# Two more gate masks of a block-sparse attention turned by transposing transfers, in a new instruction order

## The chip, the cores and the metric

The kernel runs on one core of one Trainium2 chip. The core has TensorE (matrix products), VectorE, ScalarE, GpSimd, and SyncE, which here only issues transfers; each works through its own instruction stream in order, and semaphores tie the streams together. Sixteen DMA engines move data. The metric is device time in microseconds; one execution was also profiled. On the pages PE is TensorE, PEld its weight loads, DVE VectorE, ACT ScalarE, POOL GpSimd and SP SyncE, and a q behind a name is an engine's sequencer or queue.

## The reference

The input is q, k and v of 4 batches, 8 heads, 768 positions and 64 dimensions, and two weight matrices, w_in (512 x 2048) and w_out (2048 x 512). First comes an attention in which each query sees only some blocks of 64 keys, and then a two-layer network with a tanh-approximated GELU:

```python
k_rep = k.reshape(B, H, n_blocks, block, D).mean(axis=3)
gate_scores = np.einsum('bhsd,bhnd->bhsn', q, k_rep)
gate_scores = np.where(causal, gate_scores, -1000000000.0)
own_block = pos // block
top_idx = np.argsort(gate_scores, axis=-1)[..., -top_k:]     # top_k = 3
# mask: the chosen blocks and the own block, and causal within
scores = scale * np.matmul(q, k.transpose(0, 1, 3, 2))
scores = np.where(mask, scores, -1000000000.0)
attn = softmax(scores)
out = np.matmul(attn, v)                                     # heads side by side: x, 3072 x 512
h = x @ w_in
g = 0.5 * h * (1.0 + np.tanh(c * (h + 0.044715 * h * h * h)))
return g @ w_out
```

## The kernel before, in words

**Tiles and stages.** The work goes in pairs of heads: pair p holds heads 2(p mod 4) and the next one of batch p div 4, so pairs 0 to 3 are batch 0, 4 to 7 batch 1, and so on to 15. `pre(p)` prepares a pair: k and q are turned so that the head dimension lies in the partitions, k is summed by blocks into `ks` and `ksb`, TensorE makes the gate scores (L700, "the gate product"), VectorE turns them by 32 x 32 blocks (L716), adds the causal term (L723), finds the third largest by MAX8 (L732), compares (L733), and writes the gate mask `madd` (L737), 128 queries by 10 groups of 64 columns, 12 of them used, in fp16. The mask must then be turned too, so that block numbers lie in the partitions; it is copied into rows 64 to 75 of `qT` (L370 or L366, `qT<-bank` or `qT<-mT`), under the 64 rows of q, and meets there a constant pattern in the same rows of `kT`. So the score product (L1060) adds the mask by itself. `heads(p)` makes scores (L1060), exponentials on ScalarE (L1073), the triangle of the diagonal blocks on GpSimd (L1087), and the product with v (L1099); VectorE normalises (L982, L983), and the result is turned into `xT`, by TensorE (L1002) or by a transposing transfer (L1007). Batch 0 is done by `heads2` with lines L877, L896, L922, L945, L963 and L964 for the same steps. For batch 0, k and q are turned by TensorE (L559, L566, with `ident` and `identk`, and copied from PSUM by L366 or L370); later pairs are turned on VectorE (L586) and summed there (L634).

Per batch follow two stages: `s1` (L1136, 384-column products of w_in, and GELU on ScalarE, L1148), and the product with w_out: `s2_plain` for batch 0 (L1336, 512 columns) and `s2` for the others (L1386, 256 columns, in the seven-product scheme of Strassen, with additions on VectorE, L1323 and L1435). Batch 3's first layer uses the seven-product scheme in part (L1225).

**Two ways to turn the mask.** In `pre`, for pairs from 4 on, a flag `byPE` chooses. With it, `mask` issues five transposes on TensorE (L770) into a PSUM bank, and the copies read PSUM. Without it, `mask_dma` (L777) issues one transposing transfer on SyncE's queue from `madd` into a tile `mT` of two buffers in SBUF, and the copies read that. Before, `byPE` holds for pairs 4 to 7, batch 1.

**Loads.** SyncE issues nearly all transfers. The 24 head loads of batch 0 (pairs 0 to 3, k, q and v, two heads each; L406, L441) come first, four of them on ScalarE's queue. GpSimd issues the weights (L474, converting to fp16): w_in behind a small copy (L472) that reads the last v of batch 0 and so waits for it, w_out later in GpSimd's order. SyncE then copies a marker out of w_in (L1581), which waits until w_in has landed, and goes on with the loads of pair 4 and later (L412, L406).

**What sets the order.** Nothing is scheduled while the kernel is built: `Plan.run` walks a written list `ORDER` of operation numbers (1661 that emit instructions), takes the buffer of each tile from a second list `BUFFER`, and, where an operation can go to more than one engine, the engine from a table `ENGINE`. Each engine gets its instructions in the order of the list. Costs and priorities stand beside each operation in the code, but have no effect here; they were for the search that wrote the lists. 34 dummy products on zeros (`warm`, L1538) are in the list as well; they write a PSUM bank that nothing reads.

Of the kernel before, what the change touches and what calls it, by code (L numbers as in the profile page):

```python
# [230 lines left out]
def kernel(  # L231
# [16 lines left out]
    HP = H // 2  # L248
# [295 lines left out]
    def pre(p):  # L544
# [255 lines left out]
        else:  # L800
            byPE = p < 2 * HP
# [752 lines left out]
    for p in range(HP):  # L1554
        pre(p)
# [85 lines left out]
```

## Time and profile before

| | |
|---|---|
| median of 3 runs | 250.69 us (250.57 to 252.19) |
| the profiled execution | 251.68 us, its span 250.0 us |
| granted TensorE clock, mean | 0.998 |
| TensorE busy | 244.1 us, 98% of the span, 2492 products |
| VectorE busy | 189.0 us, 76% |
| ScalarE busy | 178.1 us, 71% |
| GpSimd busy | 81.0 us, 32% |
| DMA | 33.01 MB, 132 GB/s in the mean |
| L770, all five-block turns of masks | 40 transposes, 3.8 us busy |
| L777, mask transfers of batches 2 and 3 | 8, issue 1.20 us in the median |

A row of a timeline gives start and length in microseconds from the span's start, the engine, the line and operation, what is written and read, how many, and in brackets the idle time ahead of it with the engine, tile and line that ended it. A row of a group gives the busy time, the mean of one in nanoseconds, and the idle time ahead. Products on TensorE overlap, so the start of a row is later than the end of the row before only where TensorE paused; the rate is read from start to start.

### The profile page before, as it was taken

Reading aid. Unit: us, or ns where it says so; the run is one execution under the profiler, and the core shown is the slowest. Engines: PE = TensorE matmul, PEld = TensorE weight load, DVE = VectorE, ACT = ScalarE, POOL = GpSimd, SP = SyncE. Lnnn points to the kernel's source line nnn. Section 1 sums busy time; section 2 is a strip of 40 time slices with the busy share of each in tenths; the row PEclk is TensorE's granted clock in tenths of the full one; section 3 lists DMA queues with packets and bytes.
Section 4 is the critical chain, followed back from the end, with each engine's and each line's share of the span. In section 5 each row is a group of like instructions: output and inputs, shape, how many; then the busy total and the mean of one; then the engine's idle time right before and its main releaser. Section 6 shows DMA issues by size and latency. Waiting matters only on the chain.

```text
span 250.0 us, 6442 instructions
## 1 busy us (share of the span) xinstructions
PE 244.1 (98%) x2492; PEld 170.0 (68%) x2492; DVE 189.0 (76%) x542; ACT 178.1 (71%) x226; POOL 81.0 (32%) x162
## 2 busy tenths in 40 slices
PE   8989999999999999999999999999999999999993
PEld 6757776554556666665778887665877887666883
DVE  3799861050999999997998997998968583677953
ACT  2898996553799999768899875677998937657300
POOL 8546670011225875041146542300246400000000
PEclk9999999999999999999999999999999999999999
DMA  6997799999996668999978958235510330010024
GB/s 181 230 208 149 123 215 177 215 186 156 149 190 115 124 116 145 190 192 241 178 142 144 222 115 157 73 29 143 146 46 19 105 118 1 18 69 0 4 84 168
DMA packets 130479, 33.01 MB, mean 132 GB/s; under 512 B 123056, under 2 KB 126480, under 8 KB 130448
## 3 DMA queue, kind: packets, MB, share of 16 engines
q1 hardware_dynamic: 126736, 28.01, 55.1%
q0 software_dynamic: 3136, 4.19, 10.1%
q10 hardware_dynamic: 576, 0.39, 0.6%
q8 instruction: 19, 0.31, 0.5%
q14 instruction: 12, 0.10, 0.1%
HBM read 27.26 MB, written 6.29 MB: 134 GB/s over the span
## 4 chain that ended last, share of the span: by engine, by line
PE 90%; DMA 5%; DVE 3%; ACT 0%; issue 0%; POOL 0%; DVEq 0%
PE wide L1136 24%; PE bank L1386 22%; PE wide L1060 11%; PE bank L1336 8%; PE bank L1099 6%; PE wide L1225 6%; DMA w_out<-in_moe_w_out_dram 5%; PE wide L877 2%; PE bank L700 2%; PE bank L1538 2%; PE bank L566 2%; PE bank L945 2%; PE bank L770 1%; PE bank L559 1%; DVE ks L605 1%; DVE sel L732 1%
## 5 line engine op out<-in xcount | busy, mean ns | idle before, releaser
L1136 PE MATMUL wide<-xT,w_in 128*128 128x384 f16 x416 | 74.2, 326 | 0.0
L1073 ACT ACTIVATE ats<-wide 128x896 f16<-128x896 f32 x72 | 62.7, 913 | 5.4 <-PE wide L1060 4.2
L1148 ACT ACTIVATE G<-wide 128x768 f16<-128x768 f32 x52 | 42.1, 810 | 29.3 <-PE wide L1136 28.5
L1136 PEld LDWEIGHTS <-w_in 128*128 128x128 f16 x416 | 39.7, 98 | 26.8 <-issue 1.8
L1087 POOL TENSOR_SCALAR_AFFINE_SELECT ats<-ats 128x256 f16<-128x256 f16 x72 | 30.8, 438 | 57.5 <-ACT ats L1073 56.9
L1060 PE MATMUL wide<-qT,kT 76*128 76x512 f16 (+3 forms) x192 | 38.6, 305 | 0.0
L586 DVE STREAM_TRANSPOSE s<-sd 128x768 f32<-128x768 f32 x24 | 23.3, 971 | 11.7 <-DMA sd<-in_k_dram 10.2
L1386 PE MATMUL bank<-w_out,G 128*128 128x256 f16 x216 | 31.6, 272 | 0.0
L1386 PEld LDWEIGHTS <-G 128*128 128x128 f16 x288 | 27.0, 98 | 5.7
L368 POOL CAST kT<-s 64x768 f16<-64x768 f32 x19 | 16.0, 843 | 38.6 <-DVE s L586 38.2
L1336 PE MATMUL bank<-w_out,G 128*128 128x512 f16 x96 | 27.3, 379 | 0.4 <-DMA w_out<-in_moe_w_out_dram 0.4
L1435 DVE TENSOR_TENSOR osb<-bank,osb 128x512 f32<-128x512 f32 (+1 forms) x38 | 22.2, 593 | 4.7 <-PE bank L1386 3.7
L1099 PEld LDWEIGHTS <-ats 128*128 128x128 f16 x504 | 21.8, 98 | 3.8 <-POOL v L368 0.2
L1060 PEld LDWEIGHTS <-kT 76*128 76x128 f16 x192 | 17.4, 97 | 10.0 <-issue 0.3
L1099 PE MATMUL bank<-v,ats 128*128 128x65 f16 x504 | 23.8, 194 | 0.0
L1386 PEld LDWEIGHTS <-XS 128*128 128x128 f16 x216 | 20.0, 97 | 4.0
L896 ACT ACTIVATE ats<-wide 128x1024 f16<-128x1024 f32 (+3 forms) x24 | 20.6, 916 | 2.7 <-PE wide L877 2.4
L1386 PE MATMUL bank<-TS,XS 128*128 128x256 f16 x144 | 21.6, 272 | 0.0
L366 ACT CAST qT<-s 64x768 f16<-64x768 f32 x18 | 14.8, 824 | 0.2
L368 POOL CAST v<-vsd 128x768 f16<-128x768 f32 x13 | 11.4, 880 | 10.2 <-DMA vsd<-in_v_dram 10.1
L983 DVE TENSOR_TENSOR xn<-bank,zr 128x384 f16<-128x384 f32 x24 | 13.4, 557 | 0.8
L732 DVE MAX8 sel<-sel 128x8 f32<-128x12 f32 x160 | 13.3, 157 | 0.6
(123 smaller groups left out, 348.0 us busy)
## 6 DMA issues: line engine op xcount, KB each, us to landing
out_dram<-osb SPq DMA_DIRECT2D x23, 256.0 KB
vsd<-in_v_dram SPq DMA_DIRECT2D x26, 192.0 KB
sd<-in_k_dram SPq DMA_DIRECT2D x48, 96.0 KB
sd<-in_q_dram SPq DMA_DIRECT2D x48, 96.0 KB
w_in<-in_moe_w_in_dram POOLq DMA_DIRECT2D x2, 1024.0 KB, 11.0
w_out<-in_moe_w_out_dram POOLq DMA_DIRECT2D x2, 1024.0 KB, 13.9
G<-in_k_dram SPq DMA_DIRECT2D x4, 192.0 KB
G<-in_q_dram SPq DMA_DIRECT2D x4, 192.0 KB
```

The costliest lines, as they stand in the source:

```text
L368: nc.gpsimd.tensor_copy(out=out, in_=in_)
L586: nc.vector.transpose(out=T[key + "T32", p], in_=T[key, p].rearrange("p t j -> p (t j)"))
L896: nc.scalar.activation(out=T["at", u][:, :, 0:n], in_=plan.buf[("st",) + u].rearrange("p (h w) -> p h w", h=2)[:, :, 0:n], func=AF.Exp, bi ...
L1060: nc.tensor.matmul(st[:, x:e], kT16[i][h][0:76, s0:s0 + 128], qT16[i][h][0:76, s0 + (x - cb):s0 + (e - cb)], start=True, stop=True)
L1073: nc.scalar.activation(out=T["at", u][:, 0:n], in_=plan.buf[("st",) + u][:, 0:n], func=AF.Exp, bias=0.0, scale=SCALE)
L1087: nc.gpsimd.affine_select(out=dg, in_=dg, compare_op=ALU.is_ge, fill=0.0, base=0, pattern=[[0, 2], [1, 128]], channel_multiplier=-1)
L1099: nc.tensor.matmul(pvv[:, qc, 0:65], at[:, cb + (qc - jc) * 128: cb + (qc - jc + 1) * 128], v16[i][:, jc, h, :], start=(gi == 0 and jc == ...
L1136: nc.tensor.matmul(hps[:, 512 * e:512 * e + HALF], w_in16[:, ci, (2 * j + e) * 128: (2 * j + e + 1) * 128], T["xT", b][:, ci, HALF * h:HAL ...
L1148: nc.scalar.activation(out=G[:, :, h, j, :], in_=plan.buf["hps", b, j, h].rearrange("p (e w) -> p e w", e=2)[:, :, 0:HALF], func=AF.Gelu_a ...
L1336: nc.tensor.matmul(plan.buf["ops", b, ti], G[:, f % 2, 2 * ti // NC, f // 2, ti % (NC // 2) * 128:ti % (NC // 2) * 128 + 128], w_out16[:, ...
L1386: nc.tensor.matmul(dst[:, HD * h:HD * h + HD], FACT[m][0][:, j, t * 128:(t + 1) * 128], FACT[m][1][:, j, :], start=(clear and j == 0), sto ...
L1435: nc.vector.tensor_tensor(out=dst(), in0=src(), in1=other(), op=ALU.add)
```

## The change

Pairs 6 and 7 leave the TensorE way: `byPE` now holds for pairs 4 and 5 alone.

```diff
@@ pre @@
         else:
-            byPE = p < 2 * HP
+            byPE = p < HP + 2
             if byPE:
                 m = add({PE: 0.3}, mask, [sel], pr, takes=("pre", ("mk", p, 0)))
             else:
                 go = add({SP: 1.3}, mask_dma, [sel], -50,
                          takes=("mT", ("mT", p)))
                 m = add({"DMA": 0.8}, lambda _: None, [go], pr, lag=6.0)
```

The three lists are new from the first entry to the last. (All lines behind the lists stand one lower in the new file: L1136 becomes L1135.) The first entries of each:

```diff
 ORDER = [
-    1892, 1, 18, 4, 2, 9, 1893, 0, 1894, 5, 1895, 1896, 1897, 1898, 15,
+    2, 3, 18, 1894, 0, 1895, 9, 1896, 1, 1897, 22, 1898, 1899, 1900, 1901,
...
 ENGINE = {
...
     "DVE": [
-        5, 56, 145],
+        2, 3, 5, 56, 61],
     "POOL": [
-        337, 587, 588, 648, 649, 709, 710, 974, 975, 1037, 1038, 1099, 1100,
-        1161, 1162, 1427, 1428, 1552, 1615]}
+        338, 587, 588, 649, 710, 711, 977, 1039, 1040, 1101, 1102, 1163,
+        1164, 1429, 1430, 1492, 1554, 1555, 1617]}
```

What the new lists make of the streams, counted in the plan's operations (an operation can be several instructions): TensorE 875 (877 before), VectorE 301 (291), ScalarE 213 (220), GpSimd 129 (132), SyncE 143 (141). Of the places that matter below:

| | before | after |
|---|---|---|
| L1136 products ahead of the first L1336 | 48 | 38 |
| dummy products ahead of the first L1136 / behind the first L1336 | 34 / 0 | 31 / 3 |
| GpSimd operations between the issue of w_in and of w_out | 8 | 2 |
| clearing of constants (L524 to L529) of pairs 0 and 1 | GpSimd | VectorE, ahead of the copy into `identk` (L290) |
| copies of turned q and k from PSUM, batch 0 | 13 on ScalarE, 3 on VectorE | 9 on ScalarE, 7 on VectorE |
| SyncE's first issues | k of pair 1, k of pair 0 | k and q of pair 1 (first halves), k of pair 0 |
| VectorE operations between pair 6's mask and its first copy into `qT` | 1 | 7 |
| the same for pair 7 | 1 | 6 |

307 rows, old and new, of tables (BUFFER, ENGINE, ORDER) are left out of this document.

## The prediction

> **What bounds the kernel now.** I read the page's first two parts, then the chain of work that ended last, then the busy time by stages, and then TensorE's timeline where the chain leaves TensorE.
>
> ```profile
> span 250.0 us, 6442 instructions
> PE 244.1 (98%) x2492; PEld 170.0 (68%) x2492; DVE 189.0 (76%) x542; ACT 178.1 (71%) x226; POOL 81.0 (32%) x162
> PE 90%; DMA 5%; DVE 3%; ACT 0%; issue 0%; POOL 0%; DVEq 0%
> ...
> 34.00 11.57 DMA w_out<-in_moe_w_out_dram
> 100.06 15.06 PE wide L1136 x92
> 230.03 16.20 PE bank L1386 x148
> ```
>
> The last three rows are pieces of the chain (start, length, what). TensorE has 90% of the chain, and one transfer has 5%: w_out, on which the chain leaves TensorE until 45.57. Whether TensorE had slack behind that point, the table by stages tells (length, then busy time of TensorE, its weight loads, VectorE, ScalarE, GpSimd, clock, DMA share, GB/s):
>
> ```profile
> 11.00:36.30 25.30, 24.61 (x439) 18.11 (x439) 22.28 (x86) 22.64 (x32) 15.36 (x26) 1.00 0.93 176
> 36.30:45.57 9.27, 8.95 (x80) 5.69 (x78) 1.47 (x4) 6.54 (x9) 0.66 (x2) 1.00 1.21 187
> 45.57:96.20 50.63, 50.59 (x457) 29.21 (x457) 35.69 (x103) 38.94 (x49) 19.99 (x37) 1.00 0.89 152
> 45.57:246.30 200.73, 200.59 (x1882) 138.54 (x1881) 158.58 (x416) 143.60 (x179) 56.40 (x103) 1.00 0.60 120
> ```
>
> From 45.57 to its last product at 246.30 TensorE is busy 200.59 of 200.73 us, at clock 1.00. A busy row is no proof of full rate, but the chain's long pieces give 15.06/92 = 0.164 us for a 384-column matmul and 16.20/148 = 0.109 us for a 256-column one, and the short pieces agree. So behind 45.57 the end is work divided by rate: **the span is the moment of the first w_out product, plus the TensorE work still to do then, plus a tail of 250.0 - 246.3 = 3.7 us**. I need three things of the change: TensorE work removed, work left at that moment, and whether new waits appear.
>
> **TensorE work removed.** The two mask turns of pairs 6 and 7 are five transposes each (L770); here each stands with its successor:
>
> ```profile
> 79.81 0.44 PE L770 MATMUL bank<-ident,madd 128*128 128x128 f16 x5
> 80.09 0.54 PE L1060 MATMUL wide<-qT,kT 76*128 76x512 f16 x2
> ...
> 87.90 0.44 PE L770 MATMUL bank<-ident,madd 128*128 128x128 f16 x5
> 88.19 0.59 PE L1336 MATMUL bank<-w_out,G 128*128 128x512 f16 x2
> ```
>
> Start to start, 0.28 and 0.29: **-0.57 us**, in a stage with no slack, so it counts in full.
>
> **The new order: work left at the first w_out product.** This is where I expect the change to be decided.
>
> ```profile
> 24.67 0.19 POOL L472 COPY after_in<-vsd 1x16 f32<-1x16 f32 x1 [0.72 <-DMA vsd<-in_v_dram]
> 34.00 1.78 POOL L474 DMA_DIRECT2D w_out<-in_moe_w_out_dram  x2
> 39.24 0.57 SPq L1581 DMA_DIRECT2D after_in<-w_in x1
> 36.30 0.81 PE L1136 MATMUL wide<-xT,w_in 128*128 128x384 f16 x4
> 45.61 0.38 PE L1336 MATMUL bank<-w_out,G 128*128 128x512 f16 x1 [0.36 <-DMA w_out<-in_moe_w_out_dram]
> ```
>
> GpSimd starts w_in when the last v of batch 0 has landed (24.67); w_in is whole by 39.24, where SyncE's marker copy that waits for it starts; the first half of w_out is there at 45.57. TensorE had waited 0.36 us. In the old order the first L1336 stands behind 48 L1136 matmuls, in the new one behind 38. Ten are left for afterwards: 10 x 0.164 = **+1.64 us**, if w_out lands when it did. And three of the 34 dummy matmuls (L1538, 256 columns), all ahead of the first L1136 before, now stand behind the first L1336, where nothing hides them: 3 x 0.109 = **+0.33**.
>
> When does w_out land? In the new GpSimd order its start stands two operations behind w_in's, not eight, so some 6 us earlier. But w_in's start still waits for the same last load, the 24 head loads ahead of it are the same bytes, and w_out was issued at 34.00, 5 us ahead of w_in's end, so its queue was not empty. What an earlier start could recover is a dip where w_in ends:
>
> ```profile
> 36.00:40.00 4.00, 4.00 (x53) 2.88 (x52) 1.39 (x4) 3.36 (x6) 0.81 (x2) 1.00 1.11 171
> 40.00:44.00 4.00, 4.00 (x29) 2.47 (x27) 0.36 (x1) 2.37 (x4) 0.00 (x0) 1.00 1.23 199
> ```
>
> 171 against 199 GB/s over 4 us is 0.56 us of transfer. Bounds 0 and -0.56 (a loss is excluded as long as the last v lands at its time); I take **-0.28**, the middle, since nothing shows what makes the dip: w_out at 45.3.
>
> Does TensorE get there by 45.3? Before, it arrived at 45.61 - 0.36 = 45.25; with ten matmuls fewer ahead that is 43.6. Against this, the opening got heavier on VectorE, which is busy 22.28 of 25.30 us there:
>
> ```profile
> 1.63 0.33 DVE L525 MEMSET madd<- 128x320 uint32 x1
> 2.01 0.19 DVE L529 MEMSET qT<- 12x64 uint32 x2
> 2.23 1.15 DVE L290 COPY identk<-ident 128x384 f32<-128x384 f32 x1
> 4.38 3.43 PE L566 MATMUL bank<-identk,G 128*64 128x128 f32 x36
> 22.04 0.55 DVE L370 COPY s<-bank 128x384 f32<-128x384 f32 x1
> 23.28 0.49 DVE L370 COPY XS<-bank 128x640 f16<-128x640 f16 x1
> 24.98 0.55 DVE L370 CAST v<-TS 128x768 f16<-128x768 f32 x1
> 28.36 0.28 DVE L737 SCALAR_TENSOR_TENSOR madd<-sel,ownm 128x120 f16<-128x120 f32 x1
> ```
>
> Until pair 3's gate mask (28.36) it now does four more 0.55 us copies of turned q and k, and one 0.49 copy and one 0.55 cast less: 2.20 - 1.04 = +1.16. It also clears two pairs' constants, once GpSimd's, ahead of the identk copy at 2.23. The one clearing that stands there now takes from 1.63 to 2.20, so two more are about 1.2 us; the copy then ends at 4.6 instead of 3.4, and L566 starts some 0.2 to 0.4 late. Together 43.6 + 1.16 + 0.4 = 45.1: just inside w_out's 45.3. So I let the transfer set the moment, with 0.2 us of cover; if that is gone, each further microsecond costs one (third rival).
>
> **The mask on SyncE.** What takes the place of the ten transposes:
>
> ```profile
> L370 DVE COPY qT<-mT 12x640 f16<-12x640 f16 x16 | 6.0, 374 | 0.5
> L370 DVE COPY qT<-bank 12x640 f16<-12x640 f16 x6 | 2.9, 484 | 0.3
> 108.00 1.20 SPq L777 DMA_TRANSPOSE mT<-madd x1
> 113.03 0.32 DVE L370 COPY qT<-mT 12x640 f16<-12x640 f16 x1
> L586 DVE STREAM_TRANSPOSE s<-sd 128x768 f32<-128x768 f32 x24 | 23.3, 971 | 11.7 <-DMA sd<-in_k_dram 10.2
> L634 DVE TENSOR_REDUCE ks<-s 128x12 f32<-128x768 f32 x12 | 11.2, 940 | 0.1
> L983 DVE TENSOR_TENSOR xn<-bank,zr 128x384 f16<-128x384 f32 x24 | 13.4, 557 | 0.8
> L982 DVE RECIPROCAL zr<-bank 128x6 f32<-128x6 f32 x24 | 4.5, 186 | 6.0 <-PE bank L1099 5.8
> L370 DVE CAST qT<-s 64x768 f16<-64x768 f32 x6 | 3.5, 584 | 0.1
> L716 DVE STREAM_TRANSPOSE sel<-bank 128x160 f32<-128x160 f32 (+2 forms) x17 | 5.6, 333 | 9.0 <-PE bank L700 8.8
> ```
>
> The copies into qT: three on VectorE and one on ScalarE from PSUM before (3 x 0.484 on VectorE), now four on VectorE from SBUF (4 x 0.374): VectorE +0.05, ScalarE one copy less. Neither sets the end in this stage (35.69 and 38.94 busy of 50.63), so zero; if VectorE is the one that pair 7 waits for, it is 0.05. SyncE gets two issues of 1.20 us and, being in order, stops at each until VectorE has the mask: behind pair 6's stand the rest of k of pair 9, v of pair 7, k of pair 8; behind pair 7's the turning of pair 4's output, the second half of v of pair 7, q of pairs 8 and 9. These are loads for later work; I cost them at nothing, and if v of pair 7 came late its products on TensorE would wait.
>
> The turn's latency the trace does not show alone. From below it is the issue, 1.2 us; from above 5.0, since the copy at 113.03 follows the issue at 108.00 and did not wait. Between pair 6's mask and its first copy the new order has VectorE do two transposes, a reduction, a normalisation (L982 and L983), a cast and the gate's transpose: 2 x 0.971 + 0.940 + 0.743 + 0.584 + 0.333 = 4.5 us; for pair 7 it is two transposes, a reduction, two normalisations and a copy, 1.942 + 0.940 + 1.486 + 0.374 = 4.7. At 5.0 VectorE waits 0.5 and 0.3; at 1.2 not at all. The upper end is only a copy's place in a queue, so I take zero, and keep 0 to +0.8 for the range.
>
> The Trainium skill speaks against the change here: "VectorE: DVE Perf Modes", Rules for kernel authors, would have a 128x128 transpose on TensorE where PSUM will do, and the table of The three transpose paths gives 1309 ns for the DMA's against 390 ns for TensorE's. Five blocks at that price would be an estimated 6.5 us, and the row above shows at most 5.0 from issue to copy.
>
> **The sum**, against this execution's own span: 250.0 - 0.57 + 1.64 + 0.33 - 0.28 = 251.1, so +1.1 us. The order of the last operations is different, but ends as before in three half-products, one VectorE addition and a store, so the tail stays 3.7. The profiled execution took 251.68 (1.68 around its span); the three runs' median is 250.69, and I add the difference to that: **251.8 us**.
>
> **Rivals.**
>
> *Faster: the w_out wait dissolves.* If the last v landed earlier and both weights with it, by the 1.6 us that TensorE could be early, the ten matmuls would no longer be left over: -0.57 + 0.33 - 0.36 = -0.6, 250.1 us. It decides at w_out before about 44. For: the new order issues one more load before SyncE first has to wait, and w_out is asked for sooner. Against: the transfers are the same bytes at a DMA share near 0.93. A gain of 1% would need 2.5 us, which nothing here offers.
>
> *Slower in the opening.* Besides the 1.16, the new VectorE order puts both normalisations of pair 0 (0.74 each) ahead of pair 2's mask copy, where it had one; if VectorE has no pause to absorb this, pair 3's scores come up to 0.74 later still, plus ScalarE's gap. Arrival at 46.0 to 46.4 instead of 45.3, +0.7 to +1.1 on top: 252.5 to 252.9.
>
> *The mask is late.* If the turn takes all of the 5.0 us, and SyncE has another issue of 1.2 in hand when VectorE is done, the mask is there after 6.2: VectorE, in order, waits 1.7 and 1.5 us, and the first L1060 of the pair stands in TensorE's order with nothing to pass it. That gives up to 251.8 + 3.2 = 255.0, and 253.4 if half is covered. It decides at 4.5 us from mask to landing. For: every copy of the mask behind VectorE's other work. Against: the eight turns of batches 2 and 3 delayed no copy. The table of the skill named above would put it on this side too.
>
> *The change does not do what it says:* the instruction lists have ten L770 fewer and two DMA_TRANSPOSE more, so this has no chance.
>
> **How the numbers follow.** Forecast 0.52 (its own range 251.2 to 252.5); faster 0.17; slower opening 0.2; late mask 0.11. The range must leave out no more than 0.2, so it runs from 250.0, just under the faster rival, to 253.7, just over the late mask half covered. A measurement of this kernel can tell about 1% from no change: below 248.2 or above 253.2. Above lies most of the late mask and a little of the slow opening: 0.16. Below lies only what I have not seen: 0.04.
>
> **What would show it.** Right: the first L1336 again waits for w_out, longer than 0.36, at 45.0 to 45.6; then ten L1136 more between it and the gate products of pairs 8 and 9 at the end of the stage; L1386's last piece ends near 247.4; no wait of VectorE on mT, none of TensorE at pair 6 or 7. Wrong: w_out landing before 44 or after 46.5, a wait ahead of the first L1336 that names VectorE or ScalarE, or an idle stretch of TensorE behind it.

## The result, and the profile after

| | before | after |
|---|---|---|
| median | 251.75 us (250.57 to 252.56, 8 executions) | 253.03 us (252.53 to 253.97, 8 executions) |
| ratio after to before, 95% interval | | 1.0060 (1.0033 to 1.0087) |
| the profiled execution, its span | 251.68 us, 250.0 us | 253.59 us, 251.8 us |
| TensorE products | 2492 | 2482 |
| first w_out product, wait for w_out ahead of it | 45.61 us, 0.36 us | 45.23 us, 0.77 us |
| TensorE's end | 246.22 us | 247.48 us |
| remaining time: first w_out product to TensorE's end | 200.61 us | 202.25 us |
| tail: TensorE's end to the end of the span | 3.8 us | 4.3 us |

By the medians the change costs 1.28 us, by the ratio 0.6%; the prediction said 1.1. In the eight executions of this comparison the kernel before has its median at 251.75, not at the 250.69 of its first three, so what is compared is the difference; as an absolute time the 251.8 of the prediction is 1.2 low, inside its range of 250.0 to 253.7. The two profiled executions lie 1.9 us apart, further than the medians. The page of the changed kernel, its first line, the busy times and the chain by engine:

```profile
span 251.8 us, 6423 instructions
PE 244.1 (97%) x2482; PEld 168.9 (67%) x2482; DVE 196.1 (78%) x560; ACT 175.1 (70%) x219; POOL 76.0 (30%) x151
PE 79%; DMA 10%; SPq 5%; POOL 1%; ACT 1%; issue 1%; ACTq 0%; DVE 0%; POOLq 0%
```

Ten products fewer, the same busy time of TensorE, and a longer span. Next the table by stages (same columns as for the kernel before):

```profile
11.00:36.30 25.30, 24.89 (x432) 18.19 (x430) 22.49 (x89) 22.53 (x31) 14.41 (x25) 1.00 0.96 177
36.30:45.57 9.27, 8.50 (x86) 5.47 (x84) 2.59 (x6) 6.88 (x9) 0.73 (x2) 1.00 1.23 202
45.57:247.90 202.33, 201.82 (x1885) 139.00 (x1882) 163.84 (x422) 141.25 (x174) 54.67 (x103) 1.00 0.60 120
```

Behind 45.57 TensorE is as full as before; the 0.51 us of idle time in the last row are the 0.42 behind its last product and 0.09 in 202 us. So the reading "moment plus work left" still holds. VectorE's busy time in the opening, 22.49, is only 0.21 above the 22.28 of before, though three of the four further copies stand there (the fourth starts at 5.48). The places themselves, from the timelines of TensorE, GpSimd, SyncE and VectorE:

```profile
24.26 0.20 POOL L471 COPY after_in<-vsd 1x16 f32<-1x16 f32 x1 [0.68 <-DMA vsd<-in_v_dram]
27.86 1.78 POOL L473 DMA_DIRECT2D w_out<-in_moe_w_out_dram  x2
41.38 3.09 PE L1135 MATMUL wide<-xT,w_in 128*128 128x384 f16 x18
45.23 0.38 PE L1335 MATMUL bank<-w_out,G 128*128 128x512 f16 x1 [0.77 <-DMA w_out<-in_moe_w_out_dram]
48.59 0.27 PE L1537 MATMUL bank<-XS 128*128 128x256 f16 x1
78.78 1.33 SPq L776 DMA_TRANSPOSE mT<-madd  x1
83.55 0.32 DVE L369 COPY qT<-mT 12x640 f16<-12x640 f16 x1
85.89 1.25 SPq L776 DMA_TRANSPOSE mT<-madd  x1
90.44 0.67 DVE L369 COPY qT<-mT 12x640 f16<-12x640 f16 x2
244.91 2.57 PE L1385 MATMUL bank<-w_out,G 128*128 128x256 f16 x22
247.51 0.69 DVE L1434 TENSOR_TENSOR osb<-bank,osb 128x512 f32<-128x512 f32 x1 [0.23 <-PE bank L1385]
```

The first L1335 again waits for w_out, at 45.23; TensorE was there at 44.46. One of the three late dummies follows at 48.59. Each mask is copied 4.8 and 4.6 us behind its issue, and no bracket names `mT`. TensorE ends at 244.91 + 2.57 = 247.48, VectorE's last addition at 248.20.

The tail grew too. Table by stages, first of the kernel before, then of the one after, from about the end of the last store's packets to the end of the span:

```profile
248.55:250.00 1.45, 0.00 (x0) 0.00 (x0) 0.00 (x0) 0.00 (x0) 0.00 (x0) 0.61 0.01 1
```

```profile
249.85:251.80 1.95, 0.00 (x0) 0.00 (x0) 0.00 (x0) 0.00 (x0) 0.00 (x0) 0.50 0.00 0
```

No engine is busy and next to nothing is moved in either stretch (1 and 0 GB/s), and it is 0.5 us longer after. The fourteen profiles of this case, those of the experiments below included, speak against scatter between executions. The tail is 3.7 to 3.8 us in the two kernels that turn the masks of pairs 6 and 7 on TensorE (before, e2), 4.0 to 4.1 in those with the two further transfers and the old opening (e1, e3, e8, e9, e10, e12), and 4.3 to 4.5 in those with the transfers and the new opening (after, e4 to e7, e11). In e3, which differs from the kernel before in the turns alone, the transfers thus come with 0.3 us of tail. Why they do is open.

### The profile page after: what moved, and what is told of

The parts are those of the page before. It is cut to its first block, busy times and chain, and to the rows that moved or that the text cites. A ratio compares the mean times of both kernels' runs of the same rounds, so it can differ in the third digit from the quotient of the medians.

```text
span 251.8 us, 6423 instructions
## 1 busy us (share of the span) xinstructions
PE 244.1 (97%) x2482; PEld 168.9 (67%) x2482; DVE 196.1 (78%) x560; ACT 175.1 (70%) x219; POOL 76.0 (30%) x151
## 4 chain that ended last, share of the span: by engine, by line
PE 79%; DMA 10%; SPq 5%; POOL 1%; ACT 1%; issue 1%; ACTq 0%; DVE 0%; POOLq 0%
PE wide L1135 25%; PE bank L1385 22%; PE wide L1059 11%; PE bank L1335 8%; DMA w_out<-in_moe_w_out_dram 7%; PE bank L1098 6%; SPq L405 5%; PE wide L1224 5%; DMA vsd<-in_v_dram 2%; PE bank L699 2%; DMA G<-in_q_dram 2%; POOL w_in L473 1%; ACT ats L365 1%; ACT G L1248 1%; PE bank L1001 0%
## 5 line engine op out<-in xcount | busy, mean ns | idle before, releaser
L1135 PE MATMUL wide<-xT,w_in 128*128 128x384 f16 x416 | 74.6, 326 | 0.0
L1135 PEld LDWEIGHTS <-w_in 128*128 128x128 f16 x416 | 39.9, 98 | 27.4 <-issue 2.3
L1086 POOL TENSOR_SCALAR_AFFINE_SELECT ats<-ats 128x256 f16<-128x256 f16 x72 | 29.4, 419 | 58.0 <-ACT ats L1072 40.6
L1385 PE MATMUL bank<-w_out,G 128*128 128x256 f16 x216 | 33.1, 272 | 0.0
L1335 PE MATMUL bank<-w_out,G 128*128 128x512 f16 x96 | 28.4, 379 | 0.8 <-DMA w_out<-in_moe_w_out_dram 0.8
L1098 PE MATMUL bank<-v,ats 128*128 128x65 f16 x504 | 24.6, 194 | 0.0
L1385 PE MATMUL bank<-TS,XS 128*128 128x256 f16 x144 | 23.2, 272 | 0.0
L895 ACT ACTIVATE ats<-wide 128x1024 f16<-128x1024 f32 (+3 forms) x24 | 21.2, 916 | 2.2 <-PE wide L876 1.4
L367 POOL CAST v<-vsd 128x768 f16<-128x768 f32 x12 | 10.2, 852 | 11.0 <-DMA vsd<-in_v_dram 10.4
L365 ACT CAST qT<-s 64x768 f16<-64x768 f32 x16 | 13.1, 827 | 0.2
```

The lines of the kernel that those rows point to most:

```text
L367: nc.gpsimd.tensor_copy(out=out, in_=in_)
L895: nc.scalar.activation(out=T["at", u][:, :, 0:n], in_=plan.buf[("st",) + u].rearrange("p (h w) -> p h w", h=2)[:, :, 0:n], func=AF.Exp, bi ...
L1086: nc.gpsimd.affine_select(out=dg, in_=dg, compare_op=ALU.is_ge, fill=0.0, base=0, pattern=[[0, 2], [1, 128]], channel_multiplier=-1)
L1098: nc.tensor.matmul(pvv[:, qc, 0:65], at[:, cb + (qc - jc) * 128: cb + (qc - jc + 1) * 128], v16[i][:, jc, h, :], start=(gi == 0 and jc == ...
L1135: nc.tensor.matmul(hps[:, 512 * e:512 * e + HALF], w_in16[:, ci, (2 * j + e) * 128: (2 * j + e + 1) * 128], T["xT", b][:, ci, HALF * h:HAL ...
L1335: nc.tensor.matmul(plan.buf["ops", b, ti], G[:, f % 2, 2 * ti // NC, f // 2, ti % (NC // 2) * 128:ti % (NC // 2) * 128 + 128], w_out16[:, ...
```

## The experiments

In all of them "first w_out product", "remaining time" and "TensorE's end" are read as in the table above; the new files have the same code with line numbers five lower than the kernel after (L1330 for L1335). `ORDER` is quoted as the part of one engine. In the order lists 433 and 434 are the first two w_out products, 1925 to 1927 the late dummies, 163 the start of w_out. The medians come from several chips; each ratio is against the kernel before on the same chip. The full table, in microseconds:

| kernel | first w_out product | its wait | remaining | TensorE's end | median | ratio to before (95%) |
|---|---|---|---|---|---|---|
| e1 | 44.75 | 0 | 204.14 | 248.89 | 254.58 | 1.0127 (1.0103 to 1.0152) |
| e2 | 45.51 | 0.77 | 202.56 | 248.07 | 252.92 | 1.0067 (1.0048 to 1.0087) |
| e3 | 44.35 | 0 | 204.82 | 249.17 | 255.93 | 1.0195 (1.0156 to 1.0235) |
| e4 | 45.66 | 0 | 200.64 | 246.30 | 252.45 | 1.0052 (1.0036 to 1.0069) |
| e5 | 45.75 | 0.85 | 202.24 | 247.99 | 254.08 | 1.0117 (1.0097 to 1.0138) |
| e6 | 45.84 | 0 | 200.31 | 246.15 | 252.20 | 1.0037 (1.0023 to 1.0050) |
| e7 | 48.21 | 0 | 200.62 | 248.83 | 255.07 | 1.0152 (1.0133 to 1.0171) |
| e8 | 45.08 | 0.56 | 202.23 | 247.31 | 253.58 | 1.0100 (1.0074 to 1.0125) |
| e9 | 44.56 | 0.30 | 202.37 | 246.93 | 253.22 | 1.0086 (1.0063 to 1.0108) |
| e10 | 45.01 | 0 | 202.38 | 247.39 | 253.12 | 1.0079 (1.0060 to 1.0099) |
| e11 | 45.31 | 0 | 200.30 | 245.61 | 251.82 | 1.0028 (1.0016 to 1.0041) |
| e12 | 46.08 | 0 | 201.51 | 247.59 | 253.70 | 1.0112 (1.0092 to 1.0131) |

### e1: the old opening with the new order behind it

```diff
 ORDER = [
-    2, 3, 18, 1894, 0, 1895, 9, 1896, 1, 1897, 22, 1898, 1899, 1900, 1901,
+    1894, 1, 18, 4, 2, 9, 1895, 0, 1896, 5, 1897, 1898, 1899, 1900, 15, 1901,
...
```

The first 408 entries are those of the kernel before, through a w_out product near 56 us (operation 470); then come the changed kernel's entries that are left.

> The instruction order of the kernel before up to about 56 us (through its first w_out products), the changed kernel's order behind that, masks of pairs 6 and 7 turned by SyncE. Theory of the prediction (the moment of the first w_out product and the work left then set the end; the turns themselves are free): first L1335 at 45.6 with a wait of 0.36 as before, 48 L1135 ahead of it, TensorE's end 246.22 - 0.57 = 245.65, time 0.57 us under the kernel before (ratio 0.998). Rival (the loss sits in the order behind the opening or in the turns): TensorE's end near 247.5 as in the changed kernel, with a pause of TensorE or a wait on mT between 56 us and the end.

The first w_out product came earlier than expected (44.75 instead of 45.6) and without a wait for w_out, but the seam broke. TensorE's timeline, and the table by stages behind it:

```profile
68.73 0.48 PE L694 MATMUL bank<-s,ksb 128*32 128x160 f32 x8 [2.09 <-ACT qT L360]
69.10:73.70 4.60, 4.60 (x24) 2.36 (x21) 4.10 (x17) 3.25 (x5) 2.04 (x5) 0.63 0.86 158
```

TensorE stood for 2.09 us behind ScalarE's copy of a mask, and right behind that the granted clock was 0.63 over 4.6 us, which costs 4.6 x 0.37 = 1.7 us more. 200.04 + 2.09 + 1.7 = 203.8 of the 204.14 are thus accounted for. Neither theory is decided; e8 and e9 mend the seam.

### e2: the new opening with the old order behind it

```diff
-            byPE = p < HP + 2
+            byPE = p < 2 * HP
```

with the first 407 entries of the changed kernel's `ORDER` (through the same w_out product), and then what is left of the list of the kernel before.

> The other half: the changed kernel's order up to about 56 us, the order of the kernel before behind that, masks of pairs 6 and 7 turned by TensorE. Theory: first L1336 at 45.2 with a wait of 0.77 as in the changed kernel, TensorE's end 247.48 + 0.57 = 248.05, time 1.8 us over the kernel before (ratio 1.007), since the whole loss lies in the opening. Rival (loss behind the opening): TensorE's end near 246.2 to 246.6.

TensorE's timeline:

```profile
45.51 0.38 PE L1330 MATMUL bank<-w_out,G 128*128 128x512 f16 x1 [0.77 <-DMA w_out<-in_moe_w_out_dram]
245.29 2.78 PE L1380 MATMUL bank<-w_out,G 128*128 128x256 f16 x24
```

TensorE's end 248.07, expected 248.05. With everything else old, the new opening alone costs the time: 202.56 is 200.61 + 1.64 + 0.33, to 0.02. The second reading is less kind to the change: with the masks on TensorE and the old order the remaining time is only 0.31 above the 202.25 of the changed kernel, not 0.57.

### e3: the turns alone, in the old order

```diff
-            byPE = p < 2 * HP
+            byPE = p < HP + 2
```

with the order lists of the kernel before; each transfer stands right behind its mask.

> The order of the kernel before, only the masks of pairs 6 and 7 turned by SyncE; VectorE's first copy of each mask stays where it was, 0.9 us (pair 6) and 0.8 us (pair 7) behind the mask's end, so that VectorE's wait on mT measures the turn. Theory of the prediction (turn of 1.2 to 5.0 us, near 2.5 from issue to landing): VectorE waits about 1.7 us twice, TensorE's first L1060 of each pair comes 1.2 us late, TensorE's end 246.22 - 0.57 + 2.4 = 248.0. Rival short turn (1.2): no wait of TensorE, end 245.65. Rival long turn (5.0): VectorE waits 4.1 us twice, TensorE's end near 253.

Timelines of SyncE, VectorE and TensorE:

```profile
67.35 1.68 SPq L406 DMA_DIRECT2D sd<-in_k_dram  x3
78.36 1.31 SPq L771 DMA_TRANSPOSE mT<-madd  x1
80.75 3.62 SPq L406 DMA_DIRECT2D sd<-in_k_dram  x5
81.07 0.32 DVE L364 COPY qT<-mT 12x640 f16<-12x640 f16 x1 [1.85 <-DMA mT<-madd]
81.54 0.54 PE L1054 MATMUL wide<-qT,kT 76*128 76x512 f16 x2 [1.20 <-DVE qT L364]
89.21 1.21 SPq L771 DMA_TRANSPOSE mT<-madd  x1
90.03 0.79 PE L1093 MATMUL bank<-v,ats 128*128 128x65 f16 x21 [1.43 <-DVE xn L977]
91.62 0.32 DVE L364 COPY qT<-mT 12x640 f16<-12x640 f16 x1 [1.74 <-DMA mT<-madd]
92.08 0.92 PE L1054 MATMUL wide<-qT,kT 76*128 76x512 f16 x6 [1.26 <-DVE qT L364]
```

A turn takes 81.07 - 78.36 = 2.7 us and 91.62 - 89.21 = 2.4 us from issue to copy; VectorE waits 1.85 and 1.74 (expected 1.7), TensorE 1.20 and 1.26 at the first score products (expected 1.2). The third pause, 1.43, was not expected: VectorE, late by then, normalises late, and the bank is not free. The five loads of k that SyncE issues at 80.75 went out at 71.30 in the kernel before:

```profile
71.30 3.83 SPq L412 DMA_DIRECT2D sd<-in_k_dram  x5
```

SyncE is in order, and stood from 69.03 to 78.36 at a transfer whose mask did not exist yet. So the late mask is a real mechanism: it costs 4.2 us of remaining time (204.82 against 200.61) where nothing covers it. In time e3 came out uneven: two executions took 254.95 and 255.01, some 4.0 over the kernel before (250.95), and two took 256.85 and 257.64, with a mean granted clock of 0.985 instead of 1.000 and 0.998.

The table of the Trainium skill that the prediction cites ("VectorE: DVE Perf Modes", The three transpose paths) gives 1309 ns for one 128x128 block by DMA; five blocks landed here in 2.4 to 2.7 us, about 0.5 us a block, and the measurement decides.

### e4: the wait for w_out filled

```diff
-    390, 433, 391, 373, 434, 374, 375, 376, 393, 394, 395, 396, 1925, 403,
+    390, 391, 373, 374, 375, 376, 433, 393, 394, 395, 396, 434, 1925, 403,
```

> The changed kernel with its first two L1335 moved behind the matmuls that they stood behind in the kernel before (first one behind ten more L1135). Theory (ten L1135 are 1.64 us, the wait of 0.77 is filled): no wait for w_out, first L1335 at 46.1 instead of 45.23, TensorE's end 247.48 - 0.77 = 246.71, time 0.8 us under the changed kernel, so about 0.5 over the kernel before. Rival (something else sets TensorE's pace behind 45 us, ScalarE's gelus or the PSUM tiles): the wait reappears within the next 10 us under another name, TensorE's end 247.5.

TensorE's timeline:

```profile
45.66 0.38 PE L1330 MATMUL bank<-w_out,G 128*128 128x512 f16 x1
243.73 2.57 PE L1380 MATMUL bank<-w_out,G 128*128 128x256 f16 x22
```

The wait is gone and does not come back; the remaining time falls by 1.61 (expected 1.64), the end by 1.18 (0.77 expected; TensorE got there 0.4 earlier than in the profile of after). So the ten matmuls left over are the largest term of the remaining time, as predicted. The kernel is still 0.5% slower than before, and now its arrival sets the moment: 45.66 with 48 L1130 ahead, where the old opening arrived between 44.26 and 45.25 in before, e1, e3, e8 and e9 (first product less its wait).

The expected gain in time is not seen: the ratio is 1.0052 against 1.0060 for the changed kernel, with intervals that overlap, and the kernel is 1.5 us over the one before (250.95 on this chip), where 0.5 was expected; 0.5 of the 1.5 is its longer tail. The 1.64 of the ten matmuls can't come back in full. Put back ahead, they would bring the changed kernel's TensorE to w_out at 44.46 + 1.64 = 46.10, 0.85 behind the 45.25 of before; only the wait of 0.77 is there to be filled. So the wait for w_out had hidden that the new opening is late.

### e5: w_out asked for later

```diff
-    157, 231, 145, 163, 270, 265, 276, 285, 299, 304, 310, 319,
+    157, 231, 145, 270, 265, 276, 285, 299, 304, 163, 310, 319,
```

> The changed kernel, only GpSimd's start of the w_out transfer moved back behind the operations that it stood behind in the kernel before (about 34 us instead of 27.9). Step (d) of the prediction (the earlier start fills a dip of the DMA rate): w_out lands 0.3 to 0.4 later, first L1335 at 45.6 with a wait of about 1.1, TensorE's end 247.9. New theory (the two runs with the late start met no wait at 44.35 and 44.75, the three with the early start had w_out at 45.2 to 45.5: the earlier start makes the first half land later, because it shares the queues with w_in and the loads): w_out is there by 44.4, the wait of 0.77 shrinks below 0.2, first L1335 at 44.5, TensorE's end 246.8. No effect of the start: 45.2 and 0.77 as it was.

Timelines of GpSimd and TensorE:

```profile
35.33 1.78 POOL L468 DMA_DIRECT2D w_out<-in_moe_w_out_dram  x2
45.75 0.38 PE L1330 MATMUL bank<-w_out,G 128*128 128x512 f16 x1 [0.85 <-DMA w_out<-in_moe_w_out_dram]
```

Asked for 7.5 us later, w_out lands 0.52 later, and TensorE's end moves by 0.51 to 247.99 (expected 247.9 by step (d)). The ratio says more, 1.0117 against 1.0060, with intervals that do not meet. So the new theory, that an early start delays w_out, falls. How much the early start gains is not shown: the traces tell when the first half of w_out landed, also where TensorE did not wait for it, and that is 44.3 to 45.6 in the six other kernels that ask late (before, e1, e3, e8, e9, e12) and 44.3 to 45.5 in the seven that ask early (after, e2, e4, e6, e7, e10, e11), against 45.7 here.

### e6: without the late dummies

```diff
-    396, 434, 1925, 403, 404, 435, 405, 436, 418, 406, 419, 437,
+    396, 434, 403, 404, 435, 405, 436, 418, 406, 419, 437,
```

and 1926 and 1927 likewise; the rest is e4. The dummies' products are read by nobody.

> The kernel of e4, without the three dummy matmuls that stand behind the first w_out product. Step (c) of the prediction (nothing hides them there): from the first L1330 to TensorE's end 200.64 - 0.33 = 200.31 us. Rival (they fill pauses of TensorE, or hold its clock up): 200.64 unchanged, or longer at a clock below 1.00.

```profile
45.84 0.38 PE L1330 MATMUL bank<-w_out,G 128*128 128x512 f16 x1
243.59 2.56 PE L1380 MATMUL bank<-w_out,G 128*128 128x256 f16 x22
```

From these two rows of TensorE's timeline: 246.15 - 45.84 = 200.31, to the hundredth. The 0.33 are real, and the clock stays at 1.00 without them.

### e7: four copies back on ScalarE

```diff
     "ACT": [
-        63, 67, 74, 85, 90, 94, 99, 101, 105, 107, 119, 139, 331, 345, 348,
+        63, 67, 72, 74, 85, 90, 94, 99, 101, 105, 107, 110, 119, 121, 130, 139,
+        331, 345, 348, 486, 504, 523, 541, 595, 596, 598, 656, 657, 719, 753,
...
```

The rest is e4.

> The kernel of e4, four copies of turned q and k of pairs 0, 2 and 3 back on ScalarE, where the kernel before had them (VectorE 4 x 0.55 = 2.2 us less in the opening). In e4 TensorE reaches the first L1330 at 45.66 without a wait, in e1 and e3 with the old opening at 44.75 and 44.35: 0.9 to 1.3 earlier with the same work ahead. Theory of the prediction's step (e) (VectorE's load in the opening makes TensorE late): first L1330 at 44.5 to 44.9, and the end as much earlier, if w_out has landed; otherwise a wait for w_out up to 45.2 to 45.5. Rival (ScalarE is as full there, 22.5 of 25.3 us busy; or the loads set the pace): first L1330 at 45.5 or later.

TensorE's timeline:

```profile
19.21 0.68 PE L939 MATMUL bank<-v,ats 128*128 128x65 f16 x16 [0.95 <-ACT s L360]
30.30 0.41 PE L939 MATMUL bank<-v,ats 128*128 128x65 f16 x8 [1.35 <-ACT XS L360]
48.21 0.38 PE L1330 MATMUL bank<-w_out,G 128*128 128x512 f16 x1
```

2.5 us later, with pauses that name ScalarE's copies: in this order ScalarE has no room for them. What the four copies cost on VectorE the run does not tell, since it moved the load and did not take it away. The timelines tell more. From the first score product to TensorE's arrival at w_out, with 1.64 added where ten matmuls were left over, it is 33.7 to 34.3 us in six profiles of the old opening (before, e1, e3, e8, e9, e10) and 33.7 to 34.8 in six of the new one (after, e2, e4, e5, e6, e11). And the write of pair 3's mask, behind all these copies, starts at 29.56 in the changed kernel and at 28.36 in the one before: 1.20 late, where the first score product is already 1.22 late (e11). So behind the first score product the copies add nothing that can be seen.

### e8: the seam of e1, first mend

One engine entry of e1 (348, the second mask copy of pair 4) goes from ScalarE to VectorE.

```diff
     "ACT": [
-        63, 67, 72, 74, 85, 90, 94, 99, 101, 110, 119, 121, 130, 139, 345, 348,
-        349, 449, 486, 504, 523, 541, 595, 596, 598, 656, 657, 719, 753, 933,
+        63, 67, 72, 74, 85, 90, 94, 99, 101, 110, 119, 121, 130, 139, 345, 349,
+        449, 486, 504, 523, 541, 595, 596, 598, 656, 657, 719, 753, 933, 984,
...
```

> The kernel of e1, with one copy moved: at the seam of the two orders e1 had both mask copies of pair 4 on ScalarE, the second one behind the table load, and TensorE waited 2.09 us for it (68.73); here the second is on VectorE, as in the kernel before. Theory: no pause of TensorE behind the first w_out product, clock 1.00 throughout, from the first L1330 to TensorE's end 200.61 - 0.57 = 200.04 us, time 0.57 under the kernel before (ratio 0.998), 2 us under the changed one. Rival (the clock dip and the rest of e1's loss were not the pause's): 201 to 204 us as in e1 less 2.09.

```profile
68.83 0.48 PE L694 MATMUL bank<-s,ksb 128*32 128x160 f32 x8 [1.85 <-DVE qT L364]
```

TensorE's timeline shows the same pause under another engine's name: the two orders put pair 4's mask and pair 5's gate into one bank. The clock stayed at 1.00 here, so 200.04 + 1.85 leaves 0.34 of the 202.23. Of that, 0.27 is in the 96 L1330, which took 21.22 us instead of 20.95 in the kernel before (summed from start to start, pauses left out).

### e9: the seam, second mend

```diff
 BUFFER = [
...
-    0, 2, 3, 0, 0, 0, 4, 1, 1, 0, 3, 0, 1, 1, 5, 0, 2, 1, 2, 0, 1, 0, 0, 1, 0,
+    0, 2, 3, 0, 1, 1, 4, 0, 1, 1, 3, 0, 0, 0, 5, 1, 2, 0, 2, 0, 1, 0, 1, 1, 1,
...
```

Behind the seam, PSUM banks 0 and 1, and the two wide tiles, change places; otherwise e8.

> The kernel of e8 with the PSUM banks 0 and 1 (and the two wide tiles) exchanged behind the seam: in e8 and e1 the gate of pair 5 came into the bank of pair 4's mask, which the two orders had placed differently, and TensorE waited 1.85 and 2.09 us for the mask's copy. So this is at last the opening of the kernel before with the changed kernel's order and turns behind it. Theory: no pause of TensorE behind the first w_out product, from there to TensorE's end 200.61 - 0.57 = 200.04 us, time 0.57 under the kernel before (ratio 0.998). Rival (the changed order behind the opening is worse by itself): more than 200.6 us.

TensorE's timeline:

```profile
44.56 0.38 PE L1330 MATMUL bank<-w_out,G 128*128 128x512 f16 x1 [0.30 <-DMA w_out<-in_moe_w_out_dram]
67.79 0.48 PE L694 MATMUL bank<-s,ksb 128*32 128x160 f32 x8 [1.19 <-DVE s L580]
71.31 0.45 PE L764 MATMUL bank<-ident,madd 128*128 128x128 f16 x5 [0.48 <-DVE madd L731]
244.37 2.56 PE L1380 MATMUL bank<-w_out,G 128*128 128x256 f16 x22
```

The moment is the old one, and two pauses of 1.67 us in all are left at the seam, now behind VectorE. Without them the remaining time would be 200.70: the theory's 200.04 is missed by 0.66. In the same sums 0.60 of it is in the 96 L1330 (21.55 instead of 20.95); why they took longer is not shown. A splice of two orders is a poor tool here.

### e10: e9 with w_out asked for early

```diff
-    157, 231, 265, 270, 285, 276, 61, 304, 299, 163, 310,
+    157, 231, 163, 265, 270, 285, 276, 61, 304, 299, 310,
```

> The kernel of e9, with GpSimd's start of the w_out transfer moved up behind w_in's and one operation (about 27 us instead of 33). From e5, where the same move back by 7.5 us made w_out land 0.52 later: w_out 0.3 to 0.5 earlier than in e9, no wait ahead of the first L1330, which comes when TensorE arrives (44.4 to 45.2); time 0.2 to 0.4 under e9 (ratio 0.996 to 0.997). Rival (GpSimd's 1.78 us of issuing hold up the masked probabilities of pair 2): first L1330 at 45.5 or later.

The wait of 0.30 is gone and the first half of w_out landed 0.26 earlier (44.26 against 44.52), but TensorE arrived at 45.01, not at e9's 44.26, and the remaining time is the same to 0.01. The executions of one opening differ by as much, so the run does not tell whether the earlier start gained anything; the expected 0.2 to 0.4 in time is not seen (253.12 against 253.22).

### e11: k of pair 0 ahead of q of pair 1

The changed kernel puts one load of pair 1's q ahead of the last four loads of k of pair 0. First the changed kernel's timelines of SyncE and TensorE:

```profile
1.34 0.53 SPq L405 DMA_DIRECT2D G<-in_q_dram  x1
1.91 2.59 SPq L440 DMA_DIRECT2D G<-in_k_dram  x4
6.22 1.27 PE L565 MATMUL bank<-identk,G 128*64 128x134 f32 x14 [0.77 <-DMA G<-in_k_dram]
12.20 0.28 PE L876 MATMUL wide<-XS,XS 64*128 64x256 f16 x2
```

The first score product starts at 12.20. In the kernel before it starts at:

```profile
10.98 0.28 PE L877 MATMUL wide<-XS,XS 64*128 64x256 f16 x2
```

On e6, SyncE's order:

```diff
-    18, 22, 6, 12, 23,
+    18, 6, 12, 22, 23,
```

> The kernel of e6 with one load moved on SyncE: the first half of pair 1's q behind the four quarter loads of pair 0's k instead of ahead of them, as in the kernel before. In the changed kernel TensorE waits 0.77 us for k at 6.2, which the kernel before does not, and its first score matmul starts at 12.20 instead of 10.98. New theory (this one load ahead of the first k makes the new opening late, not VectorE's four more copies): first score matmul near 11.0, first L1330 at 44.6 to 44.9 instead of 45.84, or at 45.2 with a wait for w_out; TensorE's end 0.6 to 1.2 earlier. Step (e) of the prediction (VectorE's 1.16 us of copies between 12 and 36 us makes TensorE late): first L1330 at 45.5 or later without a wait.

```profile
11.43 0.28 PE L871 MATMUL wide<-XS,XS 64*128 64x256 f16 x2
45.31 0.38 PE L1330 MATMUL bank<-w_out,G 128*128 128x512 f16 x1
243.05 2.56 PE L1380 MATMUL bank<-w_out,G 128*128 128x256 f16 x22
```

Of TensorE's timeline: the first score 0.7 earlier than e6's 12.11, the first w_out product 0.53 earlier, the end 0.54, the median 0.4 (on another chip, each against its own runs of before: 1.0028 against 1.0037, intervals that overlap). Against e6 alone, the load order would be about half of the lateness. Over all profiles this is less sure: the first score product starts at 10.48 to 10.98 in the seven with the old opening and at 11.53 to 12.20 in the six with the new one, and e11's 11.43 is only 0.10 ahead of these. So it is shown that the new opening is some 1.2 us late there; what share this load has in it is not, and the rest was not found. This is the fastest version with the new order, and still behind the kernel before.

### e12: the old order, mended around the two turns

```diff
-    655, 714, 660, 708, 661,
+    655, 708, 709, 712, 714, 565, 660, 661,
```

That is VectorE's part at pair 6, against e3: between mask (655) and copies (660, 661) stand k and q of pair 7 and a normalisation. SyncE's loads of k and v go ahead of the turn, and pair 7 is treated in the same way; one of its two mask copies (723) also moves from ScalarE to VectorE.

> The kernel before with its opening and its ending untouched; the masks of pairs 6 and 7 turned by SyncE; between about 72 and 110 us the work of SyncE, VectorE and TensorE put in an order in which the loads of k and v stand ahead of each turn on SyncE, at least 3 us of VectorE's other work between a mask and its copy, and L1330 products ahead of the first score products of the pair; and the first w_out product three L1130 operations (six matmuls, 0.98 us) later, so that a wait for w_out is filled. Theory (as in e3 a turn takes 2.4 to 2.7 us; where that and the loads are covered, the ten transposes are all gain): no wait on mT and no pause of TensorE at pairs 6 and 7, from the first L1330 to TensorE's end 200.61 - 0.57 - 0.98 = 199.06 us, tail 3.8, time 0.6 to 0.9 under the kernel before (ratio 0.9965). Rival (SyncE's in-order queue makes loads or turns late whatever their order): a wait of VectorE on mT, or on sd, over 0.5 us, and TensorE's remaining time at 199.6 or above.

TensorE's timeline:

```profile
46.08 0.38 PE L1330 MATMUL bank<-w_out,G 128*128 128x512 f16 x1
83.11 0.48 PE L694 MATMUL bank<-s,ksb 128*32 128x160 f32 x8 [0.44 <-DVE xn L977]
90.58 0.54 PE L1054 MATMUL wide<-qT,kT 76*128 76x512 f16 x3 [0.41 <-ACT ats L1067]
115.77 0.48 PE L694 MATMUL bank<-s,ksb 128*32 128x160 f32 x8 [0.57 <-DVE ksb L645]
```

No wait names `mT`, so the turns are covered; but the work that covers them comes late elsewhere, and three pauses of 1.42 us in all take their place. The remaining time is 201.51 instead of 199.06. The pauses explain 1.42 of the 2.45. In the sums from start to start, 0.49 more is in the 96 L1330 (21.44 instead of 20.95) and 0.53 in the 362 L1130 behind the first w_out product (0.1651 us each instead of 0.1636); why these took longer is open. So no version that turns these masks by SyncE beat the kernel before.

## Why the prediction was right, term by term

The sign came out, and so did the step that decides, work left behind a fixed arrival of w_out. The size is close: 251.8 predicted on a median of 250.69, which is +1.1; +1.28 measured. Part of that is luck. Between the two profiles the span grew by 1.8: -0.38 at the first w_out product, +1.64 of remaining time, +0.54 of tail. In it the transposes gave half of what was forecast, and the tail, put at nothing, cost 0.5. By the prediction's own terms:

- **Ten matmuls left over, +1.64.** Right for the remaining time: 1.61 by e4, the largest term. It is not what the change can win back: with the ten ahead again the kernel is still 0.5% slower (e4), and 0.4% without the dummies as well (e6), for the opening is late and the tail longer.
- **Three dummies, +0.33.** Right: 0.33 by e6.
- **Transposes removed, -0.57.** Half of it is seen: the remaining time falls by 0.31 from e2 to the changed kernel and by 0.30 from the kernel before (200.61) to e6. The transposes did go; summed from start to start, their rows behind the first w_out product fell from 1.11 to 0.56. In the same sums the changed kernel's L1135 took 0.1641 us each instead of 0.1636, and its 96 L1335 took 0.10 more, 0.28 in all; e4, e6 and e11 have the same rates. That the new interleaving is the cause is argued, not shown.
- **w_out lands 0.28 earlier.** Right in size in the pair of profiles (0.38), but the term is smaller than the scatter, so no run shows that the earlier start is what gives it. With the old opening and the late start, the first half of w_out landed between 44.26 and 45.57; the 45.57 on which the step stood was the late end of that. e5 shows only that a start as late as 35.33 costs time.
- **TensorE arrives at 45.1, "just inside w_out's 45.3, cover 0.2".** The forecast was too late: TensorE was there at 44.46, cover 0.77. The step's mechanism failed as well. It charged VectorE's copies (1.16) and a late copy into `identk` (0.4). But between 11.00 and 36.30 VectorE's busy time rose by 0.21 only, L565 did not start late (4.28, and 4.38 for L566 before), and behind the first score product the new opening loses nothing that can be seen (e7). The lateness is there before the first score product (1.22). One load of q ahead of k, which the table of changes lists and the prediction's steps do not price, may be a part of it (e11); the rest is open.
- **The turn is covered: zero.** Right for VectorE and TensorE. The turn takes 2.4 to 2.7 us (e3), between the bounds of 1.2 and 5.0, against 4.8 and 4.6 from issue to copy.
- **SyncE's two issues: nothing.** Right for the new order, in which TensorE has no pause at pairs 6 and 7; but not a rule. In e3 the same issue in the old place held the loads by nine microseconds.
- **Tail 3.7.** Wrong by 0.5. In the fourteen profiles the tail goes with the kernel's version (3.7 to 3.8, 4.0 to 4.1, 4.3 to 4.5), so the last operations, which the step looked at, do not tell it; the cause is open. The measured +1.28 contains it.

The rivals: the first half of w_out never landed before 44 (44.26 at the earliest, in e3 and e10), so the faster one falls for the changed kernel. The slower opening did not decide, because the wait for w_out hid it; with that wait filled (e4, e6) it does decide. The late mask is real and priced by e3, but its point of decision, 4.5 us, lies 1.8 us above the turn.

## What to carry to other kernels

Where one engine is full to the end, price a reordering by the work that it leaves behind the last fixed wait: here ten matmuls pushed behind the arrival of a weight cost three times what ten removed transposes could give. Such a price holds only while the wait stands; look at what the wait hides before you count on winning it back. A transfer on SyncE's in-order queue held everything behind it until its input existed (e3, from 69.03 to 78.36 us), so look at what stands behind it in that queue, not only at its latency. And before a term of 0.3 us is argued from one profile, look how far the same moment scatters between executions; here by 1.3 us.

## What the runs showed that was not expected

A pause of TensorE can cost twice. Behind e1's 2.09 us the granted clock was 0.63 for 4.6 us (the row of e1); behind e8's pause of 1.85, and in e3, where pauses of 1.20, 1.43 and 1.26 lie between 81 and 92 us, the clock stayed at 1.00 in the profiled execution. That differs between executions of one kernel: four of e1's six have a mean clock of 0.990 to 0.993 and two of 1.000, and two of e3's four have 0.985 and took 1.8 to 2.7 us longer than the others. The Trainium skill, "TensorE: Matmul & The Clock Gate", Part 1 under What's actually happening, has the clock fall after an idle window of about 3.4 us; e1 was idle for 2.09, and TensorE was busy for all of the 6.6 us before. One case does not give the rule, but here no 3.4 us of unbroken idle time were needed.

Moving 2.2 us of copies from VectorE (22.5 of 25.3 us busy) to ScalarE (22.4 of 25.3 busy, both in e4) moved the end by 2.5 us. Both engines were equally full, so here it was the place in each one's order that counted, not the sum.
